# Key tiles of consecutive tokens, V loaded whole, one turn per pair of tiles

## The chip, the cores and the metric

The kernel runs on one core of one Trainium2 chip. The metric is the time of one execution on the device in microseconds. The core has five engines with queues of their own, each working in order: TensorE (PE for its matmuls, PEld for its weight loads), VectorE (DVE), ScalarE (ACT), GpSimd (POOL) and SyncE (SP). SP computes nothing; it issues most of the transfers, which 16 DMA engines carry out.

## The reference

A batch of 8 sequences of 2496 tokens goes through an attention without softmax, and its result through a mixture of 8 experts of which each token takes one.

```python
scores = scale * np.matmul(z, z.transpose(0, 2, 1))     # z: 8 x 2496 x 64, scale = 1 / 2496
attn = np.maximum(scores, 0.0) ** 2
out = np.matmul(attn, v)                                # v: 8 x 2496 x 256
x = (u * out).reshape(B * S, D)
logits = x @ w_gate
expert_idx = np.argmax(logits, axis=1)                  # 8 experts, 256 -> 1024 -> 256
h = np.maximum(xe @ w1[e], 0.0)
out[mask] = gate_w[mask, None] * (h @ w2[e])
```

The scores are symmetric: queries and keys are both `z`. So a square of `attn` that has been computed with some tokens as queries and others as keys serves, turned over, also where the two change places.

## The kernel before, in words

Everything that TensorE multiplies is split into a high part and the rest (`hi` and `lo`, `hl` and `lh`), so that two or three fast matmuls stand for one in full precision.

The attention part runs over batches `b`, in each over 5 chunks `c` of queries (four of 512, the last of 448), and in each chunk over 10 pairs `kp` of key tiles of 128 (a step). Two pairs belong to one chunk of keys, `cc = kp // 2`. A step has two halves:

- `scores` makes the squares of the pair, for 512 queries and 2 x 128 keys. For `cc >= c` PE computes them (L293, L294), ScalarE takes Relu and Square (L295, L296) and the high part (L298, sometimes VectorE), VectorE the rest (L300). For `cc < c` the square was computed earlier, with the places changed: it is read back from `brought`, ScalarE takes the high part (L285) and VectorE the rest (L286).
- `weighted` multiplies the pair's V by the squares into the accumulators `acc` (L319, L321, L322), 12 matmuls a step.

`scores` runs two steps ahead of `weighted` (`LA = 2`). The rings `thi`, `tlo` and `tf` have three buffers each.

Where `cc > c`, `turn` turns the squares over for later use (L255): VectorE's transpose works on blocks of 32 x 32, each tile of a pair is one instruction, and both write into a slot. After the second pair of a chunk of keys the slot is stored to memory (`scr`, L258). `bring` loads it back in four transfers that move the blocks between the groups of partitions (L266); it is issued some steps ahead, at a step that `plan` works out.

The tiles of keys are interleaved: within a chunk of 512 keys, tile `i` holds the keys `i`, `i + 4`, `i + 8` and so on (`rows_of`); in the last chunk, three tiles interleave by 3 over 384 keys and the fourth holds the last 64 keys twice. With that order the turn reads each fourth element, `tf` as `s r q`, and the square that comes back can be read in runs of 128. V's rows must have the same order, so `fetch_v` loads a pair of V in pieces: four transfers of 32 partitions in the first four chunks of keys (L134), and for the last chunk six and then four (L139 by strides of 3, L141), among them pieces of 43 and 42 rows. A loaded pair lies in `vr`, which has two buffers. `split_v` makes its high part on ScalarE (L146) and its rest on GpSimd (L148; VectorE for the first), and so frees `vr`.

For the next batch V is loaded and split during the last chunk of a batch, one pair a step, and the split of the last pair is put at the first step of chunk 0 of the next batch. In batch 0 V is loaded two pairs ahead of its use.

Other work is strewn in between, piece by piece (`bg`, `pinned`): at the end of a chunk VectorE gates the accumulators (L344), PE computes the logits, two transfers that transpose bring these to rows (`lg`, L382), VectorE reads them (L411), four more transfers turn the gated rows (L363), the rows are stored (`xrows`, L453), and GpSimd scatters the tokens' numbers into the experts' lists (`lst`, L458). The order on each engine is set by the order of the program and by a planner that simulates it; `pinned` puts a piece of work behind what stands before it on its engines. SP's queue carries V, z, u, the stores and loads of the squares, the transposing transfers and the row stores in one order.

Then follows the expert part (L739 and after), which runs over tiles of tokens; the change doesn't touch it.

Of the kernel before, what the change touches and what calls it, by code (L numbers as in the profile page):

```python
# [8 lines left out]
F32 = mybir.dt.float32  # L9
# [39 lines left out]
def fused_kernel(ctx: ExitStack, tc: tile.TileContext, zt, ut, v, wg, wcat, out):  # L49
# [77 lines left out]
    def fetch_v(b, kp):  # L127

        vr = vraw[b, kp] = sb.tile([P, 2, D], F32, name="vr", bufs=2)
        c, h = divmod(kp, 2)  # L130
        if c < NC_ - 1:
            for g in range(G):
                src = v[b, :, G * c + g, :].rearrange("(k i) d -> k i d", i=G)
                nc.sync.dma_start(vr[g * R:(g + 1) * R], src[:, 2 * h:2 * h + 2])  # L134
            return
        for i in range(2 * h, min(2 * h + 2, 3)):
            for k in range(3):
                lo, hi = -(-(k * P - i) // 3), min(P, -(-((k + 1) * P - i) // 3))
                nc.sync.dma_start(vr[lo:hi, i - 2 * h], v[b, bass.ds(3 * lo + i - k * P, hi - lo, step=3), G * c + k, :])  # L139
        if h:  # L140
            nc.sync.dma_start(vr[:, 1, :], v[b, :, NK - 1, :])  # L141

# [88 lines left out]

    def rows_of(zt_, c, i):

        if c < NC_ - 1:
            return zt_[:, i::4]
        return zt_[:, i:3 * P:3] if i < 3 else zt_[:, 3 * P:4 * P]

    turned_, brought, kept_rows = {}, {}, {}
    cycle = [0, 0]

    def turn(b, c, cc, h, a):

        if h == 0:
            tt = turned_[b, c, cc] = slot(cycle[0] % 3)
            cycle[0] += 1
        else:
            tt = turned_.pop((b, c, cc))
        t4_ = tt.rearrange("p (s r e) -> p s r e", s=G, r=4)
        for i in range(2):
            k = 2 * h + i  # L250
            if cc < NC_ - 1:
                to = t4_[:, :, :, k::4]
            else:
                to = t4_[:, :, :, k:3 * R:3] if k < 3 else t4_[:, :, :, 3 * R:]
            nc.vector.transpose(out=to, in_=a[:, i].rearrange("p (s q r) -> p s r q", s=G, r=4))  # L255
        if h:
            d = kept_rows[b, c, cc] = dram.tile([P, 2 * F], F32, name="scr", tag="scr", bufs=8)
            nc.sync.dma_start(d, tt)  # L258

    def bring(b, cc, c):  # L260

        d = kept_rows.pop((b, cc, c))
        st = slot(3 + cycle[1] % 3)
        cycle[1] += 1
        for q in range(G):
            nc.sync.dma_start(st[q * R:(q + 1) * R].rearrange("p (g e) -> p g e", g=G),  # L266
                              d.rearrange("(g q) (s e) -> s q g e", g=G, s=G)[q])
        brought[b, cc, c] = st.rearrange("p (g r e) -> p r g e", g=G, r=4)

    free = list(range(NSLOT))  # L270

    def scores(b, c, kp):
# [3 lines left out]
        if cc < c:  # L276

            st = brought[b, cc, c][:, kp % 2 * 2:kp % 2 * 2 + 2]
            if c < NC_ - 1:
                runs = [(st, slice(0, QC), G)]  # L280
            else:
                runs = [(st[:, :, :, 0:3 * R], slice(0, 3 * P), G), (st[:, :, 0:2, 3 * R:], slice(3 * P, n), 2)]
            for a, to, g in runs:
                h, l = [x[:, :, to].rearrange("p j (g e) -> p j g e", g=g) for x in (hi, lo)]
                nc.scalar.copy(h, a)  # L285
                nc.vector.tensor_tensor(l, a, h.bitcast(F32), op=ALU.subtract)  # L286
            return hi, lo
# [3 lines left out]
        for i in range(2):  # L291
            hl_k = rows_of(ztiles[b, cc][0], cc, kp % 2 * 2 + i)
            nc.tensor.matmul(ps[:, i, :n], lhsT=hl_k, rhs=hl_q[:, :n], start=True, stop=False)  # L293
# [665 lines left out]
```

## Time and profile before

| | |
|---|---|
| median of 3 runs | 2562.58 us (2561.98 to 2563.81) |
| profiled execution | 2576.18 us, span 2574.3 us |
| mean granted clock of TensorE | 0.948 |
| busy: PE, PEld, DVE | 2333.1, 1947.0, 1754.4 us |
| busy: ACT, POOL | 1446.9, 735.3 us |
| moved by DMA | 406.00 MB in 329693 packets, 201708 of them under 512 B |
| queue of SP (q1) | 298128 packets, 284.77 MB, 51.8% of the 16 engines' span |

The profile is one execution, and its durations are put against its own time, 2576.18 us, which is 13.6 us above the median of the runs. Busy times overlap between engines and between stages, so they are read stage by stage. The first gate (L344) of a chunk marks where one chunk ends and the next begins; the attention part ends at 1644.4 us. Matmuls overlap one another: their durations (about 400 ns) are longer than the distance between their starts.

### The profile page before, as it was taken

The numbers are of one execution on the slowest core, as the hardware profiler recorded it, in microseconds if no ns is written. First come the engines' busy times: TensorE is split into PE (matmuls) and PEld (weight loads), VectorE is DVE, ScalarE is ACT, GpSimd is POOL, SyncE is SP. The second block draws the span as 40 slices with busy tenths as digits, with TensorE's granted clock in tenths as the row PEclk, the third lists the DMA queues.
The fourth block names the chain that finished last, engine by engine and source line by source line (L and its number), as shares of the span: only waits on it lengthen the run. The fifth ranks groups of instructions, "written<-read, shape, count | busy, mean of one in ns | idle before, by whom it ended". The sixth has DMA issues, their size and how long they took to land.

```text
span 2574.3 us, 32216 instructions
## 1 busy us (share of the span) xinstructions
PE 2333.1 (91%) x10872; PEld 1947.0 (76%) x10872; DVE 1754.4 (68%) x3027; ACT 1446.9 (56%) x1993; POOL 735.3 (29%) x707
## 2 busy tenths in 40 slices
PE   7997987898889799789899798799999999999998
PEld 5785776687668677667678677688888888888887
DVE  6877866787777787766786786475556566556554
ACT  4755754664655575555565574345456456556554
POOL 2112113013112112112212221454445445445431
PEclk8998998999889899899899899899999999999999
DMA  5695896986878877688779589775456456547540
GB/s 161 172 185 118 216 160 105 194 176 124 191 153 152 193 165 149 177 162 153 166 170 171 129 198 201 134 177 143 129 148 171 144 153 174 150 151 188 143 138 26
DMA packets 329693, 406.00 MB, mean 158 GB/s; under 512 B 201708, under 2 KB 245498, under 8 KB 310064
## 3 DMA queue, kind: packets, MB, share of 16 engines
q1 hardware_dynamic: 298128, 284.77, 51.8%
q0 software_dynamic: 31392, 119.10, 15.9%
q8 instruction: 87, 1.43, 0.2%
q14 instruction: 86, 0.70, 0.1%
HBM read 233.67 MB, written 127.32 MB: 140 GB/s over the span
## 4 chain that ended last, share of the span: by engine, by line
PE 54%; DMA 17%; DVE 16%; issue 4%; SPq 4%; ACT 4%; POOL 1%; DVEq 0%; ACTq 0%; POOLq 0%
PE ph L735 16%; PE y L756 11%; DMA vr<-in_v_dram 7%; DMA lg<-lp 7%; PE acc L322 6%; PE acc L321 6%; PE y L758 6%; PE acc L319 6%; DVE s L255 5%; DVE tlo L300 3%; SPq L139 2%; DVE tlo L286 2%; PE ps_s L293 2%; PE ps_s L294 1%; ACT tf L295 1%
## 5 line engine op out<-in xcount | busy, mean ns | idle before, releaser
L321 PE MATMUL acc<-tlo,t 128*128 128x512 f32 (+1 forms) x1520 | 616.5, 406 | 85.0 <-DVE tlo L300 53.9
L319 PE MATMUL acc<-thi,t 128*128 128x512 f32 (+1 forms) x1600 | 603.5, 402 | 54.5 <-ACT thi L285 26.5
L322 PE MATMUL acc<-thi,t 128*128 128x512 f32 (+1 forms) x1600 | 638.3, 400 | 3.7 <-POOL t L148 3.2
L321 PEld LDWEIGHTS acc<-tlo,t 128*128 128x128 f32 x1520 | 299.2, 197 | 162.1 <-DVE tlo L300 70.9
L319 PEld LDWEIGHTS acc<-thi,t 128*128 128x128 f32 x1600 | 312.6, 197 | 120.7 <-ACT thi L285 29.6
L740 DVE SCALAR_TENSOR_TENSOR t<-ph,t 128x512 fp32r<-128x512 f32 (+1 forms) x328 | 220.8, 675 | 267.4 <-ACT t L739 265.2
L756 PE MATMUL y<-t,t 128*128 128x512 f32 x1062 | 382.3, 400 | 8.4 <-DVE tf L768 8.4
L739 ACT ACTIVATE t<-ph 128x512 fp32r<-128x512 f32 (+1 forms) x328 | 193.7, 591 | 331.1 <-PE ph L735 280.9
L735 PE MATMUL ph<-thi,t 128*128 128x512 f32 (+2 forms) x1248 | 372.0, 362 | 2.9 <-ACT thi L717 2.7
L322 PEld LDWEIGHTS acc<-thi,t 128*128 128x128 f32 x1600 | 314.4, 197 | 63.8 <-POOL t L148 4.9
L255 DVE STREAM_TRANSPOSE s<-tf 128x512 f32<-128x512 f32 x320 | 340.3, 1117 | 32.7 <-ACT tf L296 32.4
L295 ACT ACTIVATE tf<-ps_s 128x1024 f32<-128x1024 f32 (+1 forms) x240 | 241.2, 1013 | 181.8 <-DVE tlo L300 67.1
L458 POOL DMA_INDIRECT lst<-toks,posi x160 | 189.3, 1183 | 519.3 <-DVE posi L450 462.3
L286 DVE TENSOR_TENSOR tlo<-s,thi 128x768 fp32r<-128x768 f32 (+1 forms) x224 | 213.7, 978 | 120.1 <-ACT thi L285 119.3
L758 PE MATMUL y<-t,t 128*128 128x256 f32 x1062 | 288.6, 283 | 0.0
L300 DVE TENSOR_TENSOR tlo<-tf,thi 128x1024 fp32r<-128x1024 f32 (+1 forms) x200 | 244.8, 1232 | 28.4 <-ACT thi L298 27.3
L735 PEld LDWEIGHTS ph<-thi,t 128*128 128x128 f32 x1248 | 224.7, 189 | 40.4 <-ACT thi L717 3.7
L296 ACT ACTIVATE tf<-tf 128x1024 f32<-128x1024 f32 (+1 forms) x240 | 250.0, 1052 | 3.7
L756 PEld LDWEIGHTS y<-t,t 128*128 128x128 f32 x1062 | 199.4, 191 | 49.7 <-issue 8.7
L285 ACT CAST thi<-s 128x768 fp32r<-128x768 f32 (+1 forms) x224 | 166.2, 770 | 125.9 <-PE acc L322 111.4
L735 PE MATMUL ph<-tlo,t 128*128 128x512 f32 (+2 forms) x624 | 225.1, 361 | 4.3 <-DVE tlo L718 4.3
L758 PEld LDWEIGHTS y<-t,t 128*128 128x128 f32 x1062 | 203.1, 191 | 11.1
(230 smaller groups left out, 3430.0 us busy)
## 6 DMA issues: line engine op xcount, KB each, us to landing
scr<-s SPq DMA_DIRECT2D x80, 1024.0 KB
s<-scr SPq DMA_DIRECT2D x320, 256.0 KB
xrows<-rows SPq DMA_DIRECT2D x32, 544.0 KB
vr<-in_v_dram SPq DMA_DIRECT2D x256, 64.0 KB
u<-in_ut_dram SPq DMA_DIRECT2D x32, 512.0 KB
zr<-in_zt_dram SPq DMA_DIRECT2D x40, 256.0 KB
u<-in_ut_dram SPq DMA_DIRECT2D x8, 448.0 KB
xrows<-rows SPq DMA_DIRECT2D x8, 408.0 KB
```

Source lines behind the costliest of these rows:

```text
L255: nc.vector.transpose(out=to, in_=a[:, i].rearrange("p (s q r) -> p s r q", s=G, r=4))
L286: nc.vector.tensor_tensor(l, a, h.bitcast(F32), op=ALU.subtract)
L295: nc.scalar.activation(a[:, :, :n], ps[:, :, :n], AF.Relu)
L296: nc.scalar.activation(a[:, :, :n], a[:, :, :n], AF.Square)
L300: nc.vector.tensor_tensor(lo[:, :, :n], a[:, :, :n], hi[:, :, :n].bitcast(F32), op=ALU.subtract)
L319: nc.tensor.matmul(acc[d][:, :n], lhsT=vh, rhs=hi[:, i, :n], start=first and i == 0, stop=False)
L321: nc.tensor.matmul(acc[d][:, :n], lhsT=vh, rhs=lo[:, i, :n], start=False, stop=False)
L322: nc.tensor.matmul(acc[d][:, :n], lhsT=vl, rhs=hi[:, i, :n], start=False, stop=last and i == 1)
L735: nc.tensor.matmul(o, lhsT=w1[:, part, dd, fs], rhs=xx[:, dd, :n], start=p == 0, stop=p == 5)
L740: nc.vector.scalar_tensor_tensor(hl[:, :m], ph[:, :m], 0.0, hh[:, :m].bitcast(F32), op0=ALU.max, op1=ALU.subtract)
L756: nc.tensor.matmul(y, lhsT=hh[:, cs], rhs=w2[:, f % 2].rearrange("p i d -> p (i d)"), start=f == 0, stop=False)
L758: nc.tensor.matmul(y[:, 0:D], lhsT=hl[:, cs], rhs=w2[:, f % 2, 0, :], start=False, stop=f == NF - 1)
```

## The change

- A tile of keys is 128 consecutive tokens: `rows_of` goes, and the weights of the score matmuls are 128 neighbouring columns.
- V is loaded whole, one transfer for a pair in place of 4, 6 or 4; in memory both tiles of a pair lie side by side in each partition.
- The turn of a pair is one instruction over 1024 elements, which reads in order and writes its blocks of 32 with the tiles between one another.
- What was put in order by the turn is now put in order by the instructions that read the squares back (L285, L286): they read runs of 32 elements with a stride, always 1024 elements, where the last chunk had two instructions each, of 768 and 128.

```diff
     def fetch_v(b, kp):
-        vr = vraw[b, kp] = sb.tile([P, 2, D], F32, name="vr", bufs=2)
-        c, h = divmod(kp, 2)
-        if c < NC_ - 1:
-            for g in range(G):
-                src = v[b, :, G * c + g, :].rearrange("(k i) d -> k i d", i=G)
-                nc.sync.dma_start(vr[g * R:(g + 1) * R], src[:, 2 * h:2 * h + 2])
-            return
-        for i in range(2 * h, min(2 * h + 2, 3)):
-            for k in range(3):
-                lo, hi = -(-(k * P - i) // 3), min(P, -(-((k + 1) * P - i) // 3))
-                nc.sync.dma_start(vr[lo:hi, i - 2 * h], v[b, bass.ds(3 * lo + i - k * P, hi - lo, step=3), G * c + k, :])
-        if h:
-            nc.sync.dma_start(vr[:, 1, :], v[b, :, NK - 1, :])
+        vraw[b, kp] = sb.tile([P, 2, D], F32, name="vr", bufs=2)
+        nc.sync.dma_start(vraw[b, kp], v[b, :, 2 * kp:2 * kp + 2, :])
...
-    def rows_of(zt_, c, i):
-        if c < NC_ - 1:
-            return zt_[:, i::4]
-        return zt_[:, i:3 * P:3] if i < 3 else zt_[:, 3 * P:4 * P]
...
-        t4_ = tt.rearrange("p (s r e) -> p s r e", s=G, r=4)
-        for i in range(2):
-            k = 2 * h + i
-            if cc < NC_ - 1:
-                to = t4_[:, :, :, k::4]
-            else:
-                to = t4_[:, :, :, k:3 * R:3] if k < 3 else t4_[:, :, :, 3 * R:]
-            nc.vector.transpose(out=to, in_=a[:, i].rearrange("p (s q r) -> p s r q", s=G, r=4))
+        to = tt.rearrange("p (s t i k) -> p i t s k", s=G, t=4, i=4)[:, 2 * h:2 * h + 2]
+        nc.vector.transpose(out=to, in_=a.rearrange("p i (t s k) -> p i t s k", t=4, s=G))
...
-        brought[b, cc, c] = st.rearrange("p (g r e) -> p r g e", g=G, r=4)
+        brought[b, cc, c] = st.rearrange("p (g t i k) -> p t i g k", g=G, t=4, i=4)
...
-            st = brought[b, cc, c][:, kp % 2 * 2:kp % 2 * 2 + 2]
-            if c < NC_ - 1:
-                runs = [(st, slice(0, QC), G)]
-            else:
-                runs = [(st[:, :, :, 0:3 * R], slice(0, 3 * P), G), (st[:, :, 0:2, 3 * R:], slice(3 * P, n), 2)]
-            for a, to, g in runs:
-                h, l = [x[:, :, to].rearrange("p j (g e) -> p j g e", g=g) for x in (hi, lo)]
-                nc.scalar.copy(h, a)
-                nc.vector.tensor_tensor(l, a, h.bitcast(F32), op=ALU.subtract)
+            a = brought[b, cc, c][:, kp % 2 * 2:kp % 2 * 2 + 2].rearrange("p j i g k -> p (j i) g k")
+            h, l = [x.rearrange("p j (i g k) -> p (j i) g k", i=4, g=G) for x in (hi, lo)]
+            nc.scalar.copy(h, a)
+            nc.vector.tensor_tensor(l, a, h.bitcast(F32), op=ALU.subtract)
...
-            hl_k = rows_of(ztiles[b, cc][0], cc, kp % 2 * 2 + i)
+            hl_k = ztiles[b, cc][0][:, (kp % 2 * 2 + i) * P:(kp % 2 * 2 + i + 1) * P]
```

## The prediction, as put on record before the run

> **What bounds the kernel now.** I read the page first: span, granted clock, and the chain's share by line.
>
> ```profile
> span 2574.3 us, 32216 instructions
> ...
> PEclk8998998999889899899899899899999999999999
> ...
> PE ph L735 16%; PE y L756 11%; DMA vr<-in_v_dram 7%; DMA lg<-lp 7%; PE acc L322 6%; PE acc L321 6%; PE y L758 6%; PE acc L319 6%; DVE s L255 5%; DVE tlo L300 3%; SPq L139 2%; DVE tlo L286 2%; PE ps_s L293 2%; PE ps_s L294 1%; ACT tf L295 1%
> ```
>
> PE work rules the chain, but V's load holds 7%, the queueing of its pieces at L139 2% and the turns at L255 5%; the clock falls to 0.8 only in the attention part, the first 26 of 40 slices. So I cut that part by chunk of queries, at the starts of the gates (L344). The columns are the stretch, its length, busy time and count on PE, PEld, DVE, ACT and POOL, granted clock, DMA share, GB/s. The single rows are chunk 0 of batch 0, chunks 0, 3 and 4 of batch 3, and chunk 0 of batch 4. The sums are chunks 0, 1, 2, 3 and 4, each over batches 1 to 7 (chunk 4 over 0 to 6).
>
> ```profile
> 0.00:78.70 78.70, 60.30 (x198) 44.74 (x199) 53.56 (x66) 43.67 (x50) 21.18 (x36) 0.87 0.54 156
> ...
> 625.00:678.80 53.80, 41.46 (x168) 32.75 (x168) 40.05 (x62) 31.07 (x37) 10.59 (x10) 0.87 0.70 154
> ...
> 764.80:796.70 31.90, 31.90 (x146) 26.45 (x146) 22.76 (x43) 20.30 (x25) 4.97 (x5) 1.00 1.02 186
> 796.70:830.20 33.50, 30.20 (x132) 26.49 (x131) 24.47 (x41) 17.88 (x28) 13.01 (x11) 0.90 0.68 123
> ...
> 830.20:889.50 59.30, 46.23 (x187) 36.72 (x186) 41.58 (x64) 33.68 (x39) 11.66 (x12) 0.86 0.81 173
> ...
> sum 390.80, PE 301.88 PEld 239.25 DVE 285.54 ACT 225.89 POOL 76.76; mean PE 43.13 PEld 34.18 DVE 40.79 ACT 32.27 POOL 10.97
> ...
> sum 282.90, PE 248.84 PEld 202.40 DVE 217.92 ACT 166.85 POOL 37.73; mean PE 35.55 PEld 28.91 DVE 31.13 ACT 23.84 POOL 5.39
> ...
> sum 267.60, PE 243.64 PEld 197.91 DVE 199.31 ACT 156.95 POOL 41.65; mean PE 34.81 PEld 28.27 DVE 28.47 ACT 22.42 POOL 5.95
> ...
> sum 224.90, PE 222.49 PEld 184.03 DVE 163.39 ACT 142.38 POOL 38.37; mean PE 31.78 PEld 26.29 DVE 23.34 ACT 20.34 POOL 5.48
> ...
> sum 255.30, PE 221.55 PEld 193.93 DVE 176.29 ACT 137.29 POOL 88.94; mean PE 31.65 PEld 27.70 DVE 25.18 ACT 19.61 POOL 12.71
> ```
>
> Chunk 3 is what PE alone would make: busy throughout at clock 1.00, 31.90 us for 146 matmuls, 0.2185 us each. Chunk 0 takes 390.80/7 = 55.8 us, of which PE is idle (390.80 - 301.88)/7 = 12.7, and its clock is 0.87. With 168 and 187 matmuls in alternate batches, 178 on average, its floor is 178 x 0.2185 = 38.8. So 17 us a batch are lost in chunk 0, idle and at half clock. Idle per batch is 4.9 in chunk 1, 3.4 in chunk 2, 0.3 in chunk 3 and 4.8 in chunk 4.
>
> Next, who waits:
>
> ```profile
> ACT t L146 <- DMA vr<-in_v_dram: 207.7, 25, 19.2
> DVE lw L411 <- DMA lg<-lp: 123.7, 27, 11.0
> PE ps_s L293 <- ACT tf L295: 69.8, 9, 12.4
> PE acc L321 <- DVE tlo L300: 53.9, 35, 7.2
> PE acc L321 <- DVE tlo L286: 30.7, 13, 7.4
> ```
>
> Nearly all of chunk 0's big idle is one kind of wait: PE for ScalarE's L295, 9 times, 69.8 us. The timeline around 643 us in batch 3 shows why (ACT, then SP, then PE):
>
> ```profile
> 630.32 1.06 ACT L296 ACTIVATE tf<-tf 128x1024 f32<-128x1024 f32 x1
> 643.66 0.62 ACT L146 CAST t<-vr 128x512 fp32r<-128x512 f32 x1 [12.28 <-DMA vr<-in_v_dram]
> 651.59 0.62 ACT L146 CAST t<-vr 128x512 fp32r<-128x512 f32 x1 [7.31 <-DMA vr<-in_v_dram]
> ```
> ```profile
> 627.16 4.07 SPq L139 DMA_DIRECT2D vr<-in_v_dram  x6
> 631.34 1.60 SPq L453 DMA_DIRECT2D xrows<-rows  x1
> 633.04 3.46 SPq L139 DMA_DIRECT2D vr<-in_v_dram  x3
> 636.55 1.96 SPq L141 DMA_DIRECT2D vr<-in_v_dram  x1
> ```
> ```profile
> 653.60 0.82 PE L293 MATMUL ps_s<-t,t 128*128 128x512 f32 x1 [10.83 <-ACT tf L295]
> ```
>
> ScalarE stands from 631.4 to 651.6 before the casts of V pairs 8 and 9, the last chunk's pairs, which L139 and L141 load in six and four pieces. Behind those casts stand the Relu and Square of chunk 0's scores; PE runs dry after about 11 us of this and idles 10.83. That is the bound this change touches.
>
> **The change part by part.**
>
> *V whole.* 336 loads become 80 of 256 KB. The pieces of a pair today:
>
> ```profile
> vr<-in_v_dram SPq DMA_DIRECT2D x48, 43.0 KB
> ```
>
> Pairs 8 and 9 keep SP for 4.07 + 3.46 + 1.96 = 9.5 us of issue; whole they need two issues, below 0.6 each (an issue in these rows is 4.07/6 to 1.96). Landing is what the trace does not show for a whole load. The chain's rows, start and length, bound it:
>
> ```profile
> 601.92 6.82 DMA vr<-in_v_dram
> ...
> 636.55 14.94 DMA vr<-in_v_dram
> ```
>
> An ordinary pair's last piece takes 6.82 there, the last pair's 14.94. I take 6.82, since a whole load has the ordinary pairs' shape (rows of all partitions, no pieces of 43 rows). In batch 3, pair 8 issued at 627.2 lands by 634, and pair 9, still behind the xrows store at 631.34 to 632.94, issues at 633 and lands by 640. ScalarE then stands from 631.4 to 640 instead of 651.6. Its first 11 us cost PE nothing today, so the gap closes, and the clock dip with it. What is late next is small: I leave 3 us of short waits. Chunk 0: 38.8 + 3 = 41.8, a gain of 55.8 - 41.8 = 14.0, over 7 batches **98 us** (bounds: at 14.94 landing only 20.2 - 16.6 = 3.6 us a batch, 25; at best 17 x 7 = 119).
>
> [...]
>
> In chunk 4, where the next batch's V is loaded, the pieces are even (ACT, then SP):
>
> ```profile
> 607.35 0.62 ACT L146 CAST t<-vr 128x512 fp32r<-128x512 f32 x1 [9.13 <-DMA vr<-in_v_dram]
> ```
> ```profile
> 598.51 3.82 SPq L134 DMA_DIRECT2D vr<-in_v_dram  x8
> ```
>
> Two pairs take 3.82 us of issue, then under 1.2: 2 to 3 us earlier of ScalarE's 9.13. Chunk 4 loses 4.8 us idle and, at 0.90 of 33.5 us, about 3.4 to the clock: at most 8.2 x 7 = 57 us, at least 0 if memory sets the landing. I take 3 a batch, **21 us**. In batch 0 chunk 0 takes 78.7 for 198 x 0.2185 = 43.3 of PE work, each pair of V being loaded just before use; bounds 0 and 35 (all that is not PE work; the first loads stay), I take **10 us**.
>
> *Turns and weights.* The forms, mean in ns after the busy time:
>
> ```profile
> L255 DVE STREAM_TRANSPOSE s<-tf 128x512 f32<-128x512 f32 x320 | 340.3, 1117 | 32.7 <-ACT tf L296 32.4
> ...
> L319 PEld LDWEIGHTS acc<-thi,t 128*128 128x128 f32 x1600 | 312.6, 197 | 120.7 <-ACT thi L285 29.6 <-ACT t L146 13.2 <-DVE thi L298 10.8
> ...
> L300 DVE TENSOR_TENSOR tlo<-tf,thi 128x1024 fp32r<-128x1024 f32 x192 | 236.1, 1238 | 28.3 <-ACT thi L298 27.3
> ...
> L293 PEld LDWEIGHTS ps_s<-t,t 128*128 128x128 f32 x320 | 90.8, 284 | 86.6 <-ACT tf L295 79.0
> ...
> L693 DVE TENSOR_TENSOR t<-s,t 128x512 fp32r<-128x512 f32 x120 | 82.6, 689 | 29.7 <-ACT t L692 28.3
> ...
> L286 DVE TENSOR_TENSOR tlo<-s,thi 128x768 fp32r<-128x768 f32 x64 | 69.5, 1085 | 93.8 <-ACT thi L285 93.7
> ...
> L286 DVE TENSOR_TENSOR tlo<-s,thi 128x128 fp32r<-128x128 f32 x64 | 32.3, 505 | 0.0
> ```
>
> A turn of 512 reads every fourth element and takes 1117; an ordinary DVE pass over 512 takes 689, over 1024 takes 1238. Reading in order, a pair is between 1.24 (the rate of the ordinary pass) and 2 x 1.117 = 2.23 (the rate belongs to the turn). I take 1.24, because strided reading costs in the same kernel elsewhere: the scores' weights, every fourth column, load in 284, the packed ones of L319 in 197. Saved: 160 x 0.99 = 158 us of DVE, 8 in chunk 0, falling to none in chunk 4. Nearly all of it lies beside PE: DVE has 285.54/7 = 40.8 of chunk 0's 41.8, so without the saving it would have to run there without a break, for which I charge 3 us of the gain. DVE's other cover is the look-ahead of two pairs; I take **4 us** of path in chunks 1 and 2.
>
> [...]
>
> In order, the weights of the scores load faster than in 284 ns, but do they hold PE?
>
> ```profile
> 661.90 0.39 PE L293 MATMUL ps_s<-t,t 128*128 128x512 f32 x1
> ...
> 662.60 0.39 PE L294 MATMUL ps_s<-t,t 128*128 128x512 f32 x1
> ```
>
> Four score matmuls start 0.233 apart, below 0.284, so the loads overlap; at most (0.233 - 0.2185) x 960 = 14 us, I take **2 us**.
>
> *Squares read back.* L285/L286 now read runs of 32 instead of 128. In chunk 4 one pass of 1024 (1.24) replaces 1.085 + 0.505: 0.35 x 8 a batch on DVE, hidden (25.2 of 36.5 us busy); 0. If short runs cost twice, 1.24 x 8 more would give chunk 4 35 us of DVE, still under its length. Bring, store and planner of the squares keep their sizes. Matmuls, routing and the expert part stay.
>
> Sum: 98 + 21 + 10 + 4 + 2 = 135. The profiled execution took 2576.18 (span 2574.3), so 2441; it lies 13.6 above the median of the runs, so **2428**.
>
> **The rivals.** *Turn no faster* (15%): the rate is the transposer's own. Chunk 0 at 45: 11 x 7 = 77, with 21 and 10 makes 108, 2454. [...]
>
> *V's wait moves* (20%): the whole load of pair 9 lands as late as its last piece, because memory, not its shape, is slow right after the stores and list scatters around 633 us. Gain 25 in chunk 0, 10 in chunk 4 and 10 in batch 0: 45, 2518. For it: chunk 4's even pieces also waited 9.13.
>
> *The waits for lg go too* (12%): DVE, 0.99 us freer per pair, is past its backlog when L411 waits. The 53.9 + 30.7 us that PE waits for `lo` and a like half-clock loss fall by most: 80 more, 2348. Against: the 123.7 us are DMA latency, which a free DVE doesn't shorten.
>
> *Slower* (7%): the pair's turn with its four-deep destination, jumping 2 KB per block, costs twice today's two, 4.5 us. DVE then sets chunk 0: 40.8 + 8 x 2.2 + 3 = 61.4, 5.6 over now; chunk 1 31.1 + 6 x 2.2 + 3 = 47.3, 6.9 over; chunk 2 28.5 + 4 x 2.2 + 3 = 40.3, 2.1 over: 14.6 x 7 = 102, less 31: 2634. It decides from (55.8 - 3 - 40.8)/8 = 1.5 us more per pair in chunk 0. For it: no such destination in the trace; against: strided ones cost nothing visible.
>
> **How the numbers follow.** Forecast 46%, rivals 15, 20, 12 and 7%. The range 2345 to 2525 holds the forecast, its bounds (25 for 98 gives 2501) and the first three rivals; outside are the slow one and tails. What a measurement can't tell from no change is within 0.2%, 5 us. Faster 0.90: forecast and three rivals less 3% of their lower tail; same 0.03; slower 0.07.
>
> **What would show it.** Right: ACT's wait for vr falls from 207.7 below 90; the PE waits for L295 from 69.8 below 15; chunk 0 at 40 to 44 us with clock 0.95 or more; 160 turns of 1.1 to 1.3 us; `acc` and expert rows unchanged; chunks 1 and 2 as now. Wrong: turns near 2.2 us; L146 still standing over 10 us at chunk 0's start; or the idle returning at L411, so that chunks 1 to 3 lengthen by what chunk 0 lost.

## The result, and the profile after

The changed kernel takes 2427.73 us (median of 4 runs, 2421.24 to 2431.25) against 2563.19 us for the kernel before (4 runs, 2561.98 to 2563.99): a ratio of 0.9469, interval 0.9448 to 0.949, so 5.3% faster. The forecast was 2428. That the two agree says less than it seems: two terms of its sum were wrong by some 40 us and more, in opposite directions, as the experiments show.

The page of the changed kernel: span, granted clock by slice, and the chain's share by line (V's load is now L129, the turn L231, the products L290 to L293, the column of logits `lg` as before).

```profile
span 2425.0 us, 31370 instructions
...
PEclk9999998999999999999999999999999999999999
...
PE ph L706 16%; PE y L727 12%; DMA lg<-lp 9%; PE acc L293 6%; PE acc L290 6%; PE acc L292 6%; PE y L729 6%; DVE tlo L271 4%; DMA vr<-in_v_dram 3%; DVE tlo L257 2%; PE ps_s L264 2%; PE ps_s L265 2%; DVE s L231 2%; ACT tf L266 1%; POOL lst L429 1%
```

V's load fell from 7% of the chain to 3% and the queueing of its pieces is gone; the turns fell from 5% to 2%. But `lg` rose from 7% to 9%, and a list scatter (L429) has come in. The granted clock is 0.9 or more in all slices but one (0.8), 0.972 in the mean against 0.948.

The span is 149.3 us shorter, 147.1 of it in the attention part, which ends at 1497.3 us instead of 1644.4. The stretches by chunk, cut at the first gate (L315), columns as in the prediction: chunk 0 of batch 0, then the sums of chunks 0, 1, 2, 3 and 4, each over batches 1 to 7 (chunk 4 over 0 to 6).

```profile
0.00:71.20 71.20, 54.42 (x194) 37.57 (x195) 46.83 (x57) 42.73 (x50) 22.79 (x36) 0.93 0.56 172
...
sum 264.90, PE 257.60 PEld 205.63 DVE 237.72 ACT 202.63 POOL 79.39; mean PE 36.80 PEld 29.38 DVE 33.96 ACT 28.95 POOL 11.34
...
sum 248.60, PE 244.89 PEld 197.69 DVE 192.33 ACT 191.26 POOL 38.57; mean PE 34.98 PEld 28.24 DVE 27.48 ACT 27.32 POOL 5.51
...
sum 292.50, PE 265.40 PEld 212.37 DVE 195.19 ACT 182.69 POOL 45.23; mean PE 37.91 PEld 30.34 DVE 27.89 ACT 26.10 POOL 6.46
...
sum 216.70, PE 211.98 PEld 171.55 DVE 133.17 ACT 121.31 POOL 38.62; mean PE 30.28 PEld 24.51 DVE 19.02 ACT 17.33 POOL 5.52
...
sum 265.00, PE 210.49 PEld 179.88 DVE 176.09 ACT 127.53 POOL 98.31; mean PE 30.07 PEld 25.70 DVE 25.16 ACT 18.22 POOL 14.04
```

A trap first: the gate marks the boundary, and VectorE, which issues it, is faster now, so matmuls have moved between neighbouring chunks (chunk 2 has longer PE work than before). Lengths are therefore not compared chunk by chunk without care; idle time (length less PE busy) is. The five sums together went from 1421.5 us to 1287.7, which is 133.8 less. PE's idle time in them went from 183.1 to 97.3, which is 85.8, and PE's busy time for the same number of matmuls (5349 in the trace) from 1238.4 to 1190.4, which is 48.0: that goes with the clock, which in the seven chunks 0 is 0.85 to 0.91 before and 1.00 after. In the kernel before the granted clock is 0.50 (third figure from the end) in the 6.6 us after the gap of 10.83 us that the prediction shows:

```profile
653.00:659.60 6.60, 6.00 (x13) 3.92 (x14) 6.27 (x8) 6.54 (x8) 0.80 (x2) 0.50 0.33 129
```

Of the 85.8 us of idle time, by chunk:

| chunk | idle before, us | idle after, us | gain over 7 batches |
|---|---|---|---|
| 0 | 88.9 | 7.3 | +81.6 |
| 1 | 34.1 | 3.7 | +30.4 |
| 2 | 24.0 | 27.1 | -3.1 |
| 3 | 2.4 | 4.7 | -2.3 |
| 4 | 33.7 | 54.5 | -20.8 |

Chunk 0 is nearly clean, chunk 1 too, far beyond the 4 us that the prediction gave the turns, and chunk 4 is worse. The waits of the changed kernel, all engines, then PE's own:

```profile
DVE lw L382 <- DMA lg<-lp: 142.8, 47, 11.5
...
ACT t L134 <- DMA vr<-in_v_dram: 101.5, 28, 14.3
```
```profile
PE acc L290 <- ACT thi L256: 52.6, 7, 10.2
PE acc L292 <- DVE tlo L257: 27.0, 9, 6.6
PE acc L292 <- DVE tlo L271: 17.3, 14, 4.7
...
PE ps_s L264 <- ACT tf L266: 0.2, 1, 0.2
```

PE's wait for ScalarE's Relu, 69.8 us before, is 0.2. Its waits for `lo`, 53.9 and 30.7 before, are 17.3 and 27.0. What has grown is the wait for the high part of a square read back (L256), 7 times, once a batch, 26.5 us before, and VectorE's wait for `lg`, 123.7 before. ScalarE still waits 101.5 us for V.

Where, the timelines of batch 3's chunk 4 show (start, length, engine; ScalarE, then GpSimd, then SP, then PE):

```profile
750.99 0.62 ACT L134 CAST t<-vr 128x512 fp32r<-128x512 f32 x1 [12.52 <-DMA vr<-in_v_dram]
...
752.47 1.04 ACT L256 CAST thi<-s 128x1024 fp32r<-128x1024 f32 x1
```
```profile
735.16 1.34 POOL L429 DMA_INDIRECT lst<-toks,posi  x1 [0.57 <-issue]
...
740.40 1.08 POOL L429 DMA_INDIRECT lst<-toks,posi  x1 [0.30 <-issue]
741.49 2.55 POOL L136 TENSOR_TENSOR t<-vr,t 128x512 fp32r<-128x512 f32 x2
```
```profile
742.83 1.59 SPq L129 DMA_DIRECT2D vr<-in_v_dram  x2
```
```profile
753.56 1.11 PE L290 MATMUL acc<-thi,t 128*128 128x448 f32 x2 [8.43 <-ACT thi L256]
```

Four list scatters hold GpSimd from 735.16 to 741.5. Behind them stands the rest of V (L136), which frees V's buffer; only then does SP issue the next loads, at 742.83, and ScalarE's cast starts at 750.99. Behind it stands the cast of the square (L256) for which PE waits 8.43 us. The kernel before has the same order: in its batch 2 the scatters of chunk 4 run from 591.50 to 597.15, V's rest follows, and the eight pieces of the prediction's row are issued at 598.51. Over batches 0 to 6 the first late cast of V in chunk 4 comes 16.2 to 21.1 us after the gate there and 19.0 to 22.2 us after it in the changed kernel. So V is no earlier, while PE runs out of work 16.9 to 18.5 us after the gate before and 14.5 to 18.0 after. The gate is VectorE's and has itself moved, so this comparison is rough.

The load took up to 8.2 us, where the median from issue to landing is 4.1. That is the last column of the view of transfers:

```profile
vr<-in_v_dram SPq DMA_DIRECT2D x80, 256.0 KB, 4.1
...
lst<-toks,posi POOLq DMA_INDIRECT x160, 10.1
```

A list scatter is 128 numbers of 4 bytes, and it takes 10.1 us to land, longer than 256 KB of V. VectorE's big waits for `lg` also follow a set of scatters. In chunk 2 of batch 3 four of them were issued from 663.97 to 670.4, `lg` at 669.90, and VectorE reads it at 682.87:

```profile
682.87 0.51 DVE L382 COPY lw<-lg 128x64 uint16<-128x64 uint16 x2 [10.65 <-DMA lg<-lp]
```

Last the instructions that the change touched, by form (busy time, mean ns of one, idle before):

```profile
L231 DVE STREAM_TRANSPOSE s<-tf 128x1024 f32<-128x1024 f32 x160 | 197.0, 1235 | 41.3 <-ACT tf L267 41.0
...
L264 PEld LDWEIGHTS ps_s<-t,t 128*128 128x128 f32 x320 | 60.5, 189 | 15.7 <-ACT tf L266 1.6
...
L257 DVE TENSOR_TENSOR tlo<-s,thi 128x1024 fp32r<-128x1024 f32 x160 | 199.6, 1247 | 149.1 <-ACT thi L256 147.2
```

### The profile page after: what moved, and what is told of

Same layout as the page of the kernel before. It is cut to its first block, busy times and chain, and to the rows that moved or that the text cites. A ratio compares the mean times of both kernels' runs of the same rounds, so it can differ in the third digit from the quotient of the medians.

```text
span 2425.0 us, 31370 instructions
## 1 busy us (share of the span) xinstructions
PE 2274.4 (94%) x10872; PEld 1885.9 (78%) x10872; DVE 1631.3 (67%) x2803; ACT 1443.0 (60%) x1929; POOL 757.6 (31%) x707
## 4 chain that ended last, share of the span: by engine, by line
PE 57%; DVE 16%; DMA 14%; ACT 5%; issue 5%; POOL 2%; SPq 0%; DVEq 0%; ACTq 0%; POOLq 0%
PE ph L706 16%; PE y L727 12%; DMA lg<-lp 9%; PE acc L293 6%; PE acc L290 6%; PE acc L292 6%; PE y L729 6%; DVE tlo L271 4%; DMA vr<-in_v_dram 3%; DVE tlo L257 2%; PE ps_s L264 2%; PE ps_s L265 2%; DVE s L231 2%; ACT tf L266 1%; POOL lst L429 1%
## 5 line engine op out<-in xcount | busy, mean ns | idle before, releaser
L290 PE MATMUL acc<-thi,t 128*128 128x512 f32 (+1 forms) x1600 | 590.8, 396 | 68.9 <-ACT thi L256 52.6
L292 PE MATMUL acc<-tlo,t 128*128 128x512 f32 (+1 forms) x1520 | 604.2, 398 | 45.8 <-DVE tlo L257 27.0
L293 PE MATMUL acc<-thi,t 128*128 128x512 f32 (+1 forms) x1600 | 628.5, 394 | 5.6 <-POOL t L136 5.5
L290 PEld LDWEIGHTS acc<-thi,t 128*128 128x128 f32 x1600 | 308.3, 193 | 132.2 <-ACT thi L256 55.2
L292 PEld LDWEIGHTS acc<-tlo,t 128*128 128x128 f32 x1520 | 294.3, 194 | 116.2 <-DVE tlo L257 37.7
L293 PEld LDWEIGHTS acc<-thi,t 128*128 128x128 f32 x1600 | 309.1, 194 | 63.6 <-POOL t L136 7.9
L257 DVE TENSOR_TENSOR tlo<-s,thi 128x1024 fp32r<-128x1024 f32 x160 | 199.6, 1247 | 149.1 <-ACT thi L256 147.2
L271 DVE TENSOR_TENSOR tlo<-tf,thi 128x1024 fp32r<-128x1024 f32 (+1 forms) x200 | 256.1, 1283 | 39.4 <-ACT thi L269 38.2
L429 POOL DMA_INDIRECT lst<-toks,posi x160 | 203.7, 1273 | 171.2 <-DVE posi L421 104.8
L321 POOL MEMSET rows<- 128x64 int32 x40 | 7.1, 179 | 747.9 <-DMA xrows<-rows 426.1
L231 DVE STREAM_TRANSPOSE s<-tf 128x1024 f32<-128x1024 f32 x160 | 197.0, 1235 | 41.3 <-ACT tf L267 41.0
L729 PEld LDWEIGHTS y<-t,t 128*128 128x128 f32 x1062 | 202.4, 191 | 11.1
```

Of the source, the lines that this page charges most:

```text
L231: nc.vector.transpose(out=to, in_=a.rearrange("p i (t s k) -> p i t s k", t=4, s=G))
L271: nc.vector.tensor_tensor(lo[:, :, :n], a[:, :, :n], hi[:, :, :n].bitcast(F32), op=ALU.subtract)
L290: nc.tensor.matmul(acc[d][:, :n], lhsT=vh, rhs=hi[:, i, :n], start=first and i == 0, stop=False)
L292: nc.tensor.matmul(acc[d][:, :n], lhsT=vh, rhs=lo[:, i, :n], start=False, stop=False)
L293: nc.tensor.matmul(acc[d][:, :n], lhsT=vl, rhs=hi[:, i, :n], start=False, stop=last and i == 1)
L429: i = nc.gpsimd.indirect_dma_start(out=lst1, out_offset=bass.IndirectOffsetOnAxis(ap=posi[:m, j:j + 1], axis=0), in_=toks[:m, col + j:col ...
```

## The experiments

The kernels ran in three groups of four, each group on one chip with the kernel before beside it: that one took 2632.36 us in the first group, 2630.23 in the second, 2597.65 in the third, and 2563.19 beside the result. The second and third group have the same chip by their record, so the level changes from one group to another even there. Ratios are to the kernel before in the same group; between groups ratios are compared and no times, unless it is said, and these are good to about half a per cent. The theory was at first that V's load is the change, and the turns come along for nearly nothing; the rivals, that VectorE's time is worth more than that, and that V's wait is the memory's slowness after the list scatters and not the shape of the loads.

### One part alone: V whole, the rest as before

`old_order_whole_v` is the kernel before, with V laid out in memory in the interleaved order, so that one transfer brings a pair:

```diff
     def fetch_v(b, kp):
...
+        vraw[b, kp] = sb.tile([P, 2, D], F32, name="vr", bufs=2)
+        nc.sync.dma_start(vraw[b, kp], v[b, :, 2 * kp:2 * kp + 2, :])
...
-    vp = vp.reshape(B, (S + KQ) // P, P, Dm).transpose(0, 2, 1, 3)
+    vp = np.concatenate([vp[:, :4 * QC].reshape(B, 4, P, 4, Dm).transpose(0, 2, 1, 3, 4).reshape(B, P, 16, Dm),
+                         vp[:, 4 * QC:4 * QC + 3 * P].reshape(B, P, 3, Dm),
+                         vp[:, 4 * QC + 3 * P:].reshape(B, P, 1, Dm)], axis=2)
```

> The kernel before, with its interleaved tiles, its two strided turns a pair and its reads of the squares, but with V laid out in memory in that order, so that a pair is one transfer of 256 KB. Theory (the pieces of V, above all those of 43 rows, are what ScalarE waited for): chunk 0 loses its idle, PE idle there under 3 us a batch at a clock of 0.95 or more, and 85 to 110 us of the gain are there without the rest of the change: about 2465 us. Rival (the turns' time on VectorE is what counts, V only stood in front of it): under 60 us of gain, over 2503 us, VectorE without a break in chunk 0. Rival (memory is slow there, whatever the shape): the wait of L295 stays over 40 us in all, over 2530 us.

Measured 2550.53 us, ratio 0.9679 (0.9642 to 0.9716): 82 us of 2632.36, just under the 85 to 110 that were expected, and about 3.2 of the change's 5.3 points. Chunk 0's sum over batches 1 to 7, PE's waits, and the turns of this kernel:

```profile
sum 286.00, PE 264.14 PEld 220.86 DVE 272.61 ACT 209.09 POOL 62.30; mean PE 37.73 PEld 31.55 DVE 38.94 ACT 29.87 POOL 8.90
```
```profile
PE acc L310 <- DVE tlo L289: 66.3, 26, 8.1
PE acc L308 <- ACT thi L274: 55.0, 7, 12.0
PE acc L310 <- DVE tlo L275: 52.9, 18, 7.9
```
```profile
L244 DVE STREAM_TRANSPOSE s<-tf 128x512 f32<-128x512 f32 x320 | 339.5, 1115 | 36.5 <-ACT tf L285 36.5
```

Chunk 0 is 286.00/7 = 40.9 us with 3.1 idle, close to the 41.8 of the forecast. But PE waits 119.2 us for `lo`, against 84.6 in the kernel before: with V out of the way VectorE is the next late one. It is busy 38.9 of chunk 0's 40.9 us. The part outside V's load is thus worth about 2 points, some 50 us, and not the forecast's 6.

### The shape of the last pairs' loads

`v_last_pieces` is the changed kernel with pairs 8 and 9 loaded in pieces of 43, 43 and 42 rows, as the kernel before did, and the last tile in one:

```diff
     def fetch_v(b, kp):
         vraw[b, kp] = sb.tile([P, 2, D], F32, name="vr", bufs=2)
-        nc.sync.dma_start(vraw[b, kp], v[b, :, 2 * kp:2 * kp + 2, :])
+        if kp < NKP - 2:
+            nc.sync.dma_start(vraw[b, kp], v[b, :, 2 * kp:2 * kp + 2, :])
+            return
+        for i in range(2):
+            cuts = (0, 43, 86, P) if kp == NKP - 2 or i == 0 else (0, P)
+            for lo, hi in zip(cuts, cuts[1:]):
+                nc.sync.dma_start(vraw[b, kp][lo:hi, i], v[b, lo:hi, 2 * kp + i, :])
```

> The changed kernel, but V pairs 8 and 9 in pieces again (three of 43, 43 and 42 rows for each tile, the last tile in one), pairs 0 to 7 whole. Theory (the shape of these pieces): the idle of chunk 0 is back, 7 to 12 us a batch with the clock down to about 0.87, 75 to 110 us slower than the changed kernel: about 2520 us. Rival (the gain comes from fewer loads in all, or from the turns): under 25 us slower, at most 2455 us.

Measured 2591.49 us, ratio 0.9843 (0.9806 to 0.988). Two pairs in ten, loaded in ten pieces instead of two, take back some 3.7 points. Chunk 0's sum, and PE's first wait:

```profile
sum 353.80, PE 259.08 PEld 206.52 DVE 235.06 ACT 198.05 POOL 81.65; mean PE 37.01 PEld 29.50 DVE 33.58 ACT 28.29 POOL 11.66
```
```profile
PE ps_s L270 <- ACT tf L272: 90.5, 9, 18.3
```

The 9 waits for the Relu are back, once a batch and more, and chunk 0 idles (353.80 - 259.08)/7 = 13.5 us a batch, more than the 7 to 12 that were expected and as in the kernel before (12.7). The cause that the prediction named, pairs 8 and 9 in the way of chunk 0's Relu, is shown.

### The order in which the turn reads

`turn_strided` is the changed kernel, but its turn reads each fourth element again; all other parts of the change stay. The squares read back then belong to other tokens, so results and routing differ:

```diff
-        nc.vector.transpose(out=to, in_=a.rearrange("p i (t s k) -> p i t s k", t=4, s=G))
+        nc.vector.transpose(out=to, in_=a.rearrange("p i (s k t) -> p i t s k", t=4, s=G))
```

> The changed kernel, but the turn of a pair reads each fourth element, as before, in its one instruction of 1024. The squares that are read back then belong to other tokens, so the result is another, the routing too, and only the attention part is compared. Theory (the read order sets the turn's rate): 2.15 to 2.3 us a turn instead of 1.235, VectorE 8 us fuller in chunk 0, and the attention part 25 to 80 us longer, most of it in chunks 0 and 1. Rival (the rate came from two instructions or from the destination): 1.2 to 1.4 us, no change. Rival (the turns lie beside PE altogether): 2.2 us, and under 10 us longer.

One run: 2541.18 us, 0.965 of the kernel before. The turn's form, and the attention part as one stretch:

```profile
L231 DVE STREAM_TRANSPOSE s<-tf 128x1024 f32<-128x1024 f32 x160 | 324.5, 2032 | 23.1 <-ACT tf L267 22.8
```
```profile
0.00:1611.90 1611.90, 1398.87 (x6045) 1111.92 (x6046) 1194.07 (x1762) 952.08 (x1069) 356.95 (x322) 0.94 0.83 169
```

The same instruction over the same 1024 elements takes 2032 ns with a stride of four and 1235 in order. And 2541.18 stands beside the 2550.53 of whole V alone, in the same group: one joined turn, packed weights for the scores and the new way of reading squares back, all of them in this kernel and none in that one, come to about 9 us together (one run here, four there that spread over 5 us). The other routing explains nothing of this: the scatters land in 9.5 us, as in the changed kernel (10.1), and the waits for V and `lg`, 118.7 and 178.6 us, are those of the control below. What differs from the control is PE's wait for `lo`, 111.4 us against 70.4. So most of what the change gains beside V is the order of the turn's reading.

`two_turns` is the counterpart: in order, but one turn for each tile, as before.

```diff
-        nc.vector.transpose(out=to, in_=a.rearrange("p i (t s k) -> p i t s k", t=4, s=G))
+        for i in range(2):
+            nc.vector.transpose(out=to[:, i], in_=a[:, i].rearrange("p (t s k) -> p t s k", t=4, s=G))
```

> The changed kernel, but a pair is turned by two instructions of 512 elements that read in order. Theory (the read order is the gain, one instruction for two is a detail): 0.6 to 0.75 us each, 1.2 to 1.5 us a pair against 1.235, under 10 us slower than the changed kernel (0.946 to 0.953 of the kernel before). Rival (half the gain is the joining): about 1.1 us each, 20 us slower or more.

```profile
L232 DVE STREAM_TRANSPOSE s<-tf 128x512 f32<-128x512 f32 x320 | 206.7, 684 | 42.0 <-ACT tf L268 41.9
```

Measured 2450.47 us, ratio 0.9436 (0.9401 to 0.9471), where the changed kernel had 0.9469 and, below, 0.9482. Two instructions take 1.37 us a pair against 1.235 for one, and nothing of it is seen in the time: joining the turns gives nothing.

### The control, and V's rest on VectorE

In the second group the changed kernel ran again, beside three variants of it (`after_again`, no edit).

> The changed kernel itself, as the control beside the next three, which have to be set against it on one chip. All theories: 0.945 to 0.950 of the kernel before.

Measured 2490.43 us, ratio 0.9482 (0.9441 to 0.9523). The gain is that of the result, though both kernels are slower here. Its attention part, and two of its waits:

```profile
0.00:1543.00 1543.00, 1377.83 (x6046) 1107.83 (x6047) 1078.38 (x1762) 950.79 (x1069) 359.86 (x322) 0.95 0.85 175
```
```profile
DVE lw L382 <- DMA lg<-lp: 183.7, 45, 13.5
...
ACT t L134 <- DMA vr<-in_v_dram: 116.3, 30, 16.5
```

Beside `turn_strided` this also shows how VectorE's time came to count (on another chip, but the kernel before took 2632 and 2630 us beside the two): of 69 us between the two attention parts, PE's idle time is 48 (213.0 against 165.2) and the clock 21 (busy 1398.87 against 1377.83).

`split_dve` takes the rest of V, for the first three pairs of each next batch, off GpSimd, where it stands behind the list scatters:

```diff
-        eng = nc.gpsimd if b or kp > 1 else nc.vector
+        eng = nc.vector if b and kp in order_of(b, 0)[:3] or not b and kp < 2 else nc.gpsimd
```

> The changed kernel, but the rest of the first three pairs of V of each next batch is taken by VectorE instead of GpSimd, so that the buffers of V in chunk 4 don't come free behind the four list scatters. Theory (memory is slow after the scatters, as the run with few rows shows, and V waits for that): V is issued some 5 us earlier but into the same slow time; PE idle in chunk 4 falls by no more than half of its 7.8 us, 0 to 30 us gain over the changed kernel. Rival (GpSimd's queue sets it): idle in chunk 4 under 2 us, 50 us gain or more.

Measured 2468.73 us, ratio 0.9387 (0.936 to 0.9414), 22 us below the control. Chunk 4, summed as before, of the control and then of `split_dve`:

```profile
sum 277.20, PE 209.59 PEld 178.60 DVE 174.36 ACT 128.10 POOL 101.44; mean PE 29.94 PEld 25.51 DVE 24.91 ACT 18.30 POOL 14.49
```
```profile
sum 237.90, PE 213.91 PEld 180.51 DVE 179.04 ACT 133.71 POOL 78.37; mean PE 30.56 PEld 25.79 DVE 25.58 ACT 19.10 POOL 11.20
```

Idle there is 24.0/7 = 3.4 us a batch; in the control it is 67.6/7 = 9.7. So V's wait in chunk 4 is partly the queue on GpSimd ahead of the buffer's release; the idle time that is left lies between the two expectations. In chunk 1 it is 3.2, where the control has 1.6, which fits the work that VectorE now has.

### What makes the memory slow: the list scatters

In `few_rows` each list scatter writes 16 numbers instead of 128; the lists stay mostly empty, and only the attention part is read. The second edit, here and in `own_line`, concerns the expert part.

```diff
-                m = min(P, n - j * P)
+                m = 16
...
-        src = xrows[0:NTOK - S, :] if which == "A" else xrows
+        src = xrows
```

> The changed kernel, but each list scatter (L429) writes 16 rows instead of up to 128, so the lists miss most tokens and the expert part does other work; only the attention part is compared. GpSimd's time for the scatters stays near 1 us each. Theory (after the scattered writes of 4 bytes all transfers are slow for about 8 us, and V in chunk 4 and lg in chunk 2 fall into that): V's loads in chunk 4 land within 5 us, PE idle in chunk 4 falls from 7.8 us a batch to 4 or less, in chunk 2 from 3.9 to under 1.5. Rival (V in chunk 4 waits for its buffers, which GpSimd frees only behind four scatters): chunk 4 stays within 2 us of 7.8.

```profile
0.00:1361.10 1361.10, 1330.68 (x6046) 1084.92 (x6047) 1086.14 (x1762) 956.41 (x1069) 333.66 (x322) 1.00 0.78 199
```
```profile
DVE lw L382 <- DMA lg<-lp: 27.1, 12, 5.2
ACT t L134 <- DMA vr<-in_v_dram: 33.6, 29, 3.4
```

One run, in the first group: the attention part takes 1361.1 us, and PE idles 30.4 us in all of it, at clock 1.00. In chunk 4 it idles 1.1 us a batch, in chunk 2 not at all. Both waits that the changed kernel was left with are small now, though GpSimd issues the same number of scatters, at 1.11 us each against 1.33 in the control. So it isn't the instructions but their writes. The writes can be dear by their number or by where they go: neighbouring tokens of one expert write neighbouring 4-byte entries of a list. Two kernels tell this apart, both with all 128 writes.

`list_spread` permutes the places within each block of 128 entries of a list, so that eight successive tokens of an expert go to eight stretches of 64 bytes:

```diff
+            nc.vector.tensor_scalar(pa, posi, 7, 4, op0=ALU.bitwise_and, op1=ALU.logical_shift_left)
+            nc.vector.tensor_scalar(pb, posi, 3, 15, op0=ALU.logical_shift_right, op1=ALU.bitwise_and)
+            nc.vector.tensor_tensor(pa, pa, pb, op=ALU.bitwise_or)
+            nc.vector.tensor_scalar(posi, posi, 7, 7, op0=ALU.logical_shift_right, op1=ALU.logical_shift_left)
+            nc.vector.tensor_tensor(posi, posi, pa, op=ALU.bitwise_or)
```

> The changed kernel, but the place of a token within its block of 128 list entries is permuted, so that 8 tokens that follow one another in an expert go to 8 different stretches of 64 bytes; the order of tokens in a tile doesn't matter to the result. Five small VectorE instructions a chunk more. Theory A (writes of 4 bytes into one stretch of 64 bytes stand in line, and that is what makes memory slow): fewer meet in a stretch at a time, the idle in chunks 4 and 2 falls by a third or more, 25 to 80 us gain over the changed kernel. Theory B (every small write costs, wherever it goes): no gain, 0 to 10 us slower.

Measured 2330.52 us, ratio 0.8864 (0.8838 to 0.8891): 160 us below the control, twice what was expected at most, and faster than both kernels. Its attention part and waits:

```profile
0.00:1389.50 1389.50, 1341.69 (x6046) 1089.88 (x6047) 1113.00 (x1951) 957.09 (x1069) 331.67 (x321) 0.99 0.78 195
```
```profile
ACT t L134 <- DMA vr<-in_v_dram: 41.0, 31, 4.8
...
DVE lw L382 <- DMA lg<-lp: 16.5, 7, 5.0
```

In chunk 4 the load of V is still issued behind the four scatters, 11.1 to 13.2 us after the gate (10.6 to 13.5 in the control), but the cast that waits for it comes 14.6 to 17.3 us after the gate instead of 19.6 to 25.0. PE idles 1.7 us a batch there, where the control has 9.7.

`own_line` puts the entries 64 bytes apart in another tensor; the lists that the expert part reads stay empty, and only the attention part is read.

```diff
-    lst1 = lst.rearrange("a b -> (a b)").unsqueeze(1)
+    lst2 = dram.tile([NROW + 1, 16 * SMALL], F32, name="lst2")
+    lst1 = lst2.rearrange("a b -> (a b)").unsqueeze(1)
...
+            nc.vector.tensor_scalar(posr, posr, 16.0, None, op0=ALU.mult)
...
-        src = xrows[0:NTOK - S, :] if which == "A" else xrows
+        src = xrows
```

> The changed kernel, but the list scatter writes its entries 64 bytes apart into another tensor, so that no two of them share a stretch of 64 bytes; the lists stay empty, the expert part does other work and only the attention part is compared. The number of writes is the same. Theory A (writes into one stretch stand in line): chunk 4 and chunk 2 lose their idle as with few rows, attention part about 1361 us as there. Theory B (the number of small writes): attention part as in the changed kernel, 1490 us or more.

```profile
0.00:1395.80 1395.80, 1340.96 (x6045) 1085.33 (x6046) 1097.61 (x1799) 961.07 (x1069) 346.81 (x321) 0.99 0.76 194
```

One run: 1395.8 us of attention, as with the spread lists (1389.5) and far from the control's 1543.0. The same number of writes takes 147 us less: it is their nearness that costs. The number may cost something too: the theory expected the 1361 us of `few_rows`, which ran on another chip, and some 35 us are left between them.

### How much of each part is the slow memory

In the third group the spread lists were put under three stages of the change. `before_spread` is the kernel before with the five lines above; `pieces_spread` is `v_last_pieces` with them; `spread_split_dve` is the changed kernel with them and with `split_dve`'s line.

> The kernel before, with nothing of the change, but with the list entries permuted within blocks of 128 as in the run list_spread. It tells how much of the wait for V's pieces was their shape and how much the slow memory after the list scatters. Theory (shape alone, as the prediction had it): PE idle in chunk 0 stays at 8 us a batch or more. Rival (slow memory alone): it falls under 2 us. If both are needed: 2 to 8 us. In all cases chunks 1, 2 and 4 lose most of their idle; 0.93 to 0.90 of the kernel before.

> The changed kernel with the list entries permuted (list_spread, 0.886 of the kernel before) and V pairs 8 and 9 in pieces of 43 and 42 rows (v_last_pieces). Without slow memory the pieces show their own price. Theory (shape): chunk 0 has 6 us or more of idle again, 0.91 to 0.93 of the kernel before. Rival (the pieces were slow only where memory was): under 2 us of idle more than list_spread's 2.3, at most 0.895.

> The changed kernel with the list entries permuted, and the rest of the first three pairs of V of a next batch on VectorE. What is left of idle in chunk 4 with list_spread is 1.8 us a batch, so at most 7 x 1.8 = 13 us can be gained if GpSimd's queue holds it; if it doesn't, nothing, or some us lost where VectorE is full in chunk 0. 0.880 to 0.890 of the kernel before.

| kernel | us (range) | ratio (interval) |
|---|---|---|
| before_spread | 2438.89 (2435.16 to 2443.27) | 0.9399 (0.9363 to 0.9435) |
| pieces_spread | 2367.13 (2365.14 to 2369.08) | 0.9119 (0.9084 to 0.9154) |
| spread_split_dve | 2327.89 (2326.34 to 2329.26) | 0.8963 (0.893 to 0.8997) |

Chunk 0's sums of the first two, and chunk 4's of the third:

```profile
sum 341.20, PE 285.71 PEld 227.68 DVE 279.69 ACT 209.23 POOL 70.30; mean PE 40.82 PEld 32.53 DVE 39.96 ACT 29.89 POOL 10.04
```
```profile
sum 308.00, PE 253.55 PEld 202.59 DVE 239.20 ACT 197.01 POOL 84.80; mean PE 36.22 PEld 28.94 DVE 34.17 ACT 28.14 POOL 12.11
```
```profile
sum 227.20, PE 212.72 PEld 184.00 DVE 189.07 ACT 140.27 POOL 80.06; mean PE 30.39 PEld 26.29 DVE 27.01 ACT 20.04 POOL 11.44
```

With the spread lists, the kernel before idles 55.5/7 = 7.9 us a batch in chunk 0, where its profile without them has 12.7; with the uneven pieces alone it is 54.5/7 = 7.8, against 2.3 in `list_spread`. The 7.9 lies at the edge between what was expected of the shape alone (8 or more) and of both causes (2 to 8). So the shape of the pieces has a price of its own: 39 us of time, from `pieces_spread` to `spread_split_dve`, which also has `split_dve`'s line. That line adds nothing any more: 2327.89 us against 2330.52 without it in the second group. The other 72 us, from `before_spread` to `pieces_spread`, are the turn's and pairs 0 to 7's together; PE's waits for `lo` go from 64.5 to 14.5 us between the two. With the slow memory the same pieces cost 0.9843 - 0.9482 = 3.6 points of 2632, some 95 us. So the shape costs more than twice as much where the memory is slow; neither explains chunk 0 alone. Two expected ratios are missed. `before_spread` stays at 0.94, where 0.93 to 0.90 were expected, and its chunk 2 keeps 20 us of idle time of 24. For `spread_split_dve`, the kernel before is faster in this group while the spread kernels take the same time. The whole change, from `before_spread` to `spread_split_dve`, is a ratio of 2327.89 / 2438.89 = 0.954, a little less of a gain than with the slow memory (0.947 and 0.948).

## Why the prediction was right, and where it was wrong

*Chunk 0, forecast 98 us.* The mechanism was right: pairs 8 and 9 held ScalarE, the Relu stood behind them, PE ran dry. The wait fell from 69.8 us to 0.2, the clock of chunk 0 is 1.00 in all seven batches, and `v_last_pieces` brings the idle time back. The size was a little low: 3 us of short waits were left in the sum, and 1.1 us remain (264.90/7 = 37.8 us for 168 matmuls, whose floor by the prediction's 0.2185 is 36.7). By that floor the gain is (17.0 - 1.1) x 7 = 111 us. The landing of 6.82 us that was taken was too long: in batch 3 the whole pairs 8 and 9 are issued at 584.30 and 586.17, and their casts start 3.1 and 4.1 us later. These issues are nearly over when the scatters begin, at 586.28; in the kernel before the pieces went out from 627.16 to 638.51, and scatters ran from 631.24 to 637.24. So part of the gain may be that whole loads leave ahead of the scatters; no run separates this from the shape.

*Batch 0, forecast 10.* 78.7 to 71.2 us: 7.5.

*Chunk 4, forecast 21.* This step failed. The prediction charged part of ScalarE's wait for V to SP's issue of eight pieces, and expected 3 us a batch from one issue. The idle time of chunk 4 rose instead, by 20.8 us over seven batches. The issue did get shorter, 1.59 us for two pairs (under 1.2 was taken), and V's cast came no earlier. The load isn't late by its issue but because its buffer comes free behind four list scatters on GpSimd (`split_dve`: 9.7 us of idle to 3.4), and because it then travels through a memory that these scatters' writes have made slow (`list_spread`: ScalarE's wait for V from 116.3 us to 41.0). The row was there before: chunk 4's even pieces waited 9.13 us, and GpSimd's scatters stood right ahead of them. It was quoted for the rival on the memory and given 20%. That rival was right about the cause in chunk 4, though it too expected a gain there; in chunk 0, where it was to decide, slow memory is a part of the idle time (12.7 to 7.9 us in `before_spread`) and the shape of the pieces the other. The sign that was set, ScalarE's wait for V below 90 us, was missed with 101.5, and this is the reason.

*Turns, forecast 4 us of path and 2 for the weights.* The duration was right: 1.24 us taken, 1.235 measured. Turns in order take 684 ns for 512 elements and 1235 for 1024, from which an estimate is 1.08 ns an element and some 130 ns a turn besides. With the stride a turn of 1024 takes 2032 ns, a factor of 1.65; why the stride costs that, no run shows. What failed is the sentence "Nearly all of it lies beside PE". VectorE's busy share was below one in each chunk, and so its saving was costed at nearly nothing; but VectorE works in bursts, and PE's waits for `lo` are where it shows. They went from 84.6 to 44.3 us, chunk 1's idle from 34.1 to 3.7, and chunk 1's granted clock, 0.92 to 1.00 before, is 1.00 in all seven batches after. The memory has a part in this: with whole V alone chunk 1 keeps 32.7 us of idle time, but the kernel before with spread lists, its turns as slow as ever, has 5.8. `old_order_whole_v` and `turn_strided`, both with the slow turn, stay at 0.968 and 0.965. The order of reading is worth about 2 points, near 50 us. The rival that the waits for `lg` go with the faster turn fell: VectorE waits 142.8 us for `lg`, more than before; that wait belongs to the memory, and `list_spread` takes it to 16.5 in place of the control's 183.7.

*Weights and squares read back, forecast 2 and 0.* Packed, the weights load in 189 ns instead of 284. Between `old_order_whole_v` and `turn_strided` lie about 9 us for these and the joined turn together. The pass that reads runs of 32 takes 1247 ns, as costed (1.24).

*The sum.* V alone: forecast 129, measured 82 us, where the kernel before took 2632. The rest: forecast 6, measured about 50. The errors cancel, and 2428 came out. The time alone would have confirmed a wrong account of a third of the gain; only the parts, run alone, show it. The uneven pieces keep a price of 39 us with the spread lists; no run shows what in their shape makes it.

*Still open.* The kernel before took 2563 to 2632 us in the four comparisons, and the changed one 2428 and 2490, while the changed kernel with spread lists took 2331 and, with `split_dve`'s line, 2328. That fits a slowness after the scatters that differs from one group of runs to another; what makes it differ was not tested. That PE comes sooner to the same late V is the likely reason why chunk 4's idle time rose, but no run shows it alone. Nor was it tested from which distance on two small writes stop hindering each other: with 64 bytes between them the attention part took 1395.8 us (`own_line`), against 1543.0 in the control.

## What to carry to other kernels

Look for transfers that come in uneven pieces, and for the cast that stands in an in-order queue behind them: what is late is not the cast but everything queued after it (here PE idled 10.83 us behind one). A busy share below one does not make an engine's time free; ask which waits on the bounding engine end at it, and count the clock after a gap (here 0.50 in the 6.6 us after those 10.83). When a sum comes out right, run its parts alone before believing it, and when large transfers are late, look at the smallest writes that were issued just ahead of them.

## What the runs showed of the hardware

In these kernels small writes to neighbouring places slowed the transfers behind them, the loads of V and the transposing transfers of `lg`: with the same writes spread, the waits for V fell from 116.3 to 41.0 us and those for `lg` from 183.7 to 16.5 (`list_spread` against its control). Scatters of 128 numbers of 4 bytes, next to one another in the lists, land in 10.1 us (median) in the changed kernel, and a load of 256 KB issued 2.4 us behind the last of four took up to 8.2 us, where the median is 4.1. With 16 numbers each they land in 4.5 us:

```profile
lst<-toks,posi POOLq DMA_INDIRECT x160, 4.5
```

The same 128 numbers, placed so that eight successive ones go to eight stretches of 64 bytes, land in 7.0 us (`spread_split_dve`) and take 160 us off a kernel of 2490 us (`list_spread`), for five small VectorE instructions a chunk. No run here shows how near writes come to hinder each other and the transfers behind them.

A VectorE transpose in order took as long as an ordinary pass (684 ns for 512 and 1235 for 1024, against 689 and 1238); with a stride of four floats it took 1115 and 2032. The scores' weights, read with a stride of four floats, loaded in 284 ns in the mean, packed in 189, and the score matmuls start 0.233 us apart with either. The timeline of the changed kernel, from the first start to the fifth:

```profile
589.78 0.40 PE L264 MATMUL ps_s<-t,t 128*128 128x512 f32 x1
...
590.71 0.39 PE L264 MATMUL ps_s<-t,t 128*128 128x512 f32 x1
```
